# Linear attention and a routed expert layer on one core: a new explicit order for four engines and the transfers, and running counts in fewer, wider matmuls

## The chip, the cores and the metric

The kernel runs on one core of a Trainium2 chip. The core has a matrix engine (TensorE, PE in the profile), three further compute engines (VectorE or DVE, ScalarE or ACT, GpSimd or POOL) and SyncE (SP), which here only issues transfers. Each engine works through its own instructions in order; they wait for each other by semaphores. The metric is the device time of one execution in microseconds.

## The reference

Inputs are q, k, v, a_re, a_im of shape (4, 8, 768, 48), that is batch B, heads H, sequence S and head size D, and the weights of an expert layer with 8 experts, of which each token uses two.

```python
mag = np.sqrt(a_re * a_re + a_im * a_im)
scale = np.minimum(mag, 0.999) / (mag + 1e-06)
a_re_n, a_im_n = a_re * scale, a_im * scale
for t in range(S):                      # a complex decay of a state per head
    new_re = ar * S_re - ai * S_im
    new_im = ar * S_im + ai * S_re
    S_re, S_im = new_re + outer(k[t], v[t]), new_im
    y[t] = q[t] @ S_re
x = y as (B * S, H * D)                 # 3072 tokens of 384 numbers
noisy = x @ w_gate + log1p(exp(x @ w_noise)) * noise
top2, top2_w = the two largest of 8 and their softmax
for e in range(8):                      # w1[e]: 384 x 1024, w2[e]: 1024 x 384
    out[mask] += top2_w * (relu(x[mask] @ w1[e]) @ w2[e])
```

## The kernel before

The sequence is cut into chunks of 128 steps: 6 groups g of 4 tiles each (one tile per batch entry), so 24 tiles n = 0 to 23. The decay is split into a logarithm of its size and a phase. For each pair of tiles m the kernel loads a (S1, S2), takes logarithms and an arctangent (A1 to A5, D1 to D5), forms running sums by a triangular matmul (P1, P2), and sines and cosines (A7, A8). For each tile it scales q and k (D9 to D11), transposes them (P3, P4; copies A11, A12), forms scores (P5a, P5b; masked by D12a, D12b), the state update (P6, D13) and the output (P7a, P7b; copy A13), and transposes that back (P8, A14) into the rows `xr` of its group. Between groups the state is scaled by decay columns that make a round trip through DRAM (S5 out, S6 in as `ecol`; then D14, D15).

When a group's rows are there, the gates follow: logits (G0 to G3), noise and the two largest (G4 to G8), weights (G9, G12a to G12e), a running count of tokens per expert over the group's tiles (G10 on TensorE, G11a, G11b) and from it the slots `sl` (G12f, G12g). Then two indirect transfers per tile from GpSimd (L571 of the profile; L*bk.g* in the code: tile b, choice k, group g) scatter the rows of 1600 bytes to `xs` in DRAM, each expert's tokens side by side: eight scatters in groups 0 to 3. Groups 4 and 5 are cut in two parts, of three tiles and of one (4b, 5b). A copy of the group's rows also goes to `xd` (S13).

The expert part loads an expert's rows from `xs` (S14 for expert 0: the first 320 slots need groups 0 to 2 alone), transposes and splits them (P21, A23, D23), and runs two matrix products (P22 and P23) with weights loaded in pieces (S20, S22) and split into a rounded part and a rest on ScalarE and VectorE (A20, D20, A22, D22). Experts 1 to 7 follow at the end without an explicit order. Transfers that fill slots that may stay empty (S11, `xs<-none`, 300 KB each, eight) and clear the output (S12, `out_dram<-zero`, 384 KB each, twelve) can stand nearly anywhere ahead of their use.

Line 207 holds `ORDER`, a list of 1270 names in one line of time. A name is a step and its number: A is ScalarE, D VectorE, P TensorE, S a transfer on SP's queue; the G steps are on VectorE but for G0, G2, G10 (TensorE) and G1, G5, G7, G9 (ScalarE). Lines 960 to 964 take each engine's names in turn and make the first instruction of each follow the last of the one before. So the table sets the order inside an engine, not the times; and of a step with several instructions, such as the two S6 transfers, only the first has to stay behind the step before. The table ends with P23.02, expert 0's third output tile, and the few steps behind it.

`PACE` (line 526) names for most scatters one ScalarE step. The scatter waits until that step has run (line 948). The anchor is a lower bound: if the slots come later than the anchor, the scatter runs when the slots are there, in GpSimd's order.

```python
for d, n in behind:
    tc.add_manual_dep(d.ins, K[n][-1].ins.name, later, reason="pace")
```

Of the kernel before, what the change touches and what calls it, by code (L numbers as in the profile page):

```python
# [77 lines left out]
def kernel(  # L78
# [8 lines left out]
    nc = tc.nc  # L87
# [108 lines left out]
    def next_psc():  # L196
# [16 lines left out]
        D10.1 A11.0 S1.4 D11.1 P2.3 A2.2 P4.0 A1.3 D1.2 P6.0 A2.3 D2.2 S2.4 S7.1 A12.0 D1.3 S3.5 S6.1 A3.2
        P3.1 D13.0 A9.2 D3.2 P5a.0 A10.2 A9.3 D2.3 S5.2 P6.1 A4.2 S7.2 P5b.0 D9.2 S10.0 A3.3 A10.3 D3.3 A11.1
        D11.2 A4.3 S7.3 P4.1 S10.1 D13.1 S3.6 A0.3 D10.2 P6.2 S6.2 D12a.0 S2.5 A5.2 S4.3 P7a.0 A12.1 D5.2 A5.3
        D13.2 P1.4 S3.7 P1.5 D5.3 A6.4 S11.1 P3.2 A6.5 D7.4 D7.5 S7.4 P1.6 A11.2 D8.2 P1.7 D12b.0 A6.6 P4.2
        D9.3 A7.2 P7b.0 A6.7 D7.6 P5a.1 A8.2 S7.5 D7.7 S12.0 P5b.1 A13.0 D12a.1 S5.3 A12.2 S4.4 D8.3 P8.0 S3.8
        D12b.1 P7a.1 A7.3 S1.5 P5a.2 D4.2 A8.3 P7b.1 D10.3 P5b.2 A14.0 A0.4 D12a.2 P2.4 D12b.2 P3.3 A13.1
        D11.3 A9.4 P2.5 A11.3 S5.4 D4.3 P7a.2 S6.3 P7b.2 A10.4 A9.5 D9.4 S11.2 P8.1 A1.4 S4.5 P4.3 S7.6 A10.5
        D10.4 S12.1 A14.1 P2.6 A12.3 S5.5 D9.5 P2.7 S1.6 A13.2 D11.4 P3.4 A2.4 S6.4 D10.5 P5a.3 A11.4 S3.9  # L220
        D1.4 P5b.3 A9.6 A1.5 P4.4 D12a.3 S5.6 S4.6 A9.7 D12b.3 S2.6 P6.3 A2.5 D2.4 S1.7 P7a.3 A10.6 S7.7 D1.5
        A12.4 P7b.3 P8.2 S11.3 D9.6 A10.7 P3.5 S6.5 A14.2 A3.4 D11.5 S4.7 P5a.4 S3.10 A11.5 D2.5 P5b.4 S2.7
        A13.3 D3.4 P4.5 A3.5 S5.7 D12a.4 G0.0 A4.4 S11.4 D3.5 S12.2 A12.5 P7a.4 D12b.4 A4.5 D4.4 P5a.5 P5b.5
        A0.5 D10.6 P7b.4 D13.3 A5.4 D4.5 P8.3 P3.6 A13.4 D5.4 S8.5 G1.0 A14.3 S3.11 G2.0 A5.5 G3.0 P1.8 S8.4
        D12a.5 S6.6 P1.9 D5.5 A6.8 P6.4 A6.9 D7.8 A11.6 D7.9 P1.10 S4.8 D11.6 S12.3 A8.4 P1.11 S3.12 D13.4
        P4.6 A6.10 S11.5 D8.4 A6.11 D7.10 P6.5 A7.4 S6.7 D7.11 P7a.5 D12b.5 A12.6 D8.5 P7b.5 A8.5 D9.7 P5a.6
        A7.5 S4.9 D13.5 S12.4 D10.7 P8.4 A0.6 S3.13 P2.8 D11.7 P3.7 A14.4 G4.0 D12a.6 A9.8 P2.9 G5.0 A10.8
# [5 lines left out]
        S11.6 D13.7 P5a.8 A14.5 S7.10 A11.9 D11.9 S6.11 P6.8 G12d.0 A3.7 D10.10 P4.9 S7.11 A14.6 D12a.8 P8.7
        S3.15 A12.9 S12.6 D3.7 G0.1 S2.8 A15.2 A14.7 S4.11 D11.10 P5b.8 G1.1 S11.7 A4.7 G2.1 G12f.0 D12b.8
        P5a.9 A0.7 D14.1 P5b.9 G12e.0 S3.16 D15.4 G12g.0 P7a.8 G3.1 D4.6 A5.6 P7b.8 D12b.9 A5.7 D5.6 P3.10
        A13.8 D12a.9 P1.12 A11.10 D13.8 P1.13 D5.7 A6.12 P4.10 D15.5 A6.13 S3.17 D7.12 P7a.9 A12.10 S1.9 D15.6
        D7.13 P1.14 D9.11 A8.6 P7b.9 A6.14 D8.6 D10.11 P5a.10 A13.9 A7.6 D7.14 P1.15 D12a.10 P8.8 A6.15 D15.7
# [15 lines left out]
        A2.11 S5.18 D12a.15 S9.8 P3.16 A9.19 G8f.2 D12b.15 A10.19 S7.18 D13.14 P7a.15 A11.16 S5.19 G8g.2 D2.10
        S4.17 P7b.15 D9.19 P4.16 S6.18 A13.15 D10.17 A3.10 P8.13 S9.9 D1.11 G9.2 P6.15 A14.13 S13.1 A12.16
        G8h.2 G0.3 G12a.2 S7.19 D2.11 G10.2 D3.10 A3.11 P3.17 D11.17 A4.10 S6.19 P5a.16 G12b.2 A11.17 G11a.2
        D3.11 P5b.16 S4.18 S3.22 A15.4 D13.15 G1.3 P4.17 A4.11 G12c.2 G11b.2 D12a.16 G2.3 P8.14 A12.17 G3.3
        G12d.2 D10.18 P8.15 A0.11 S4.19 P5a.17 G12e.2 G12f.2 D14.3 P6.16 D15.12 A5.10 G12g.2 P7a.16 D12b.16
# [941 lines left out]
```

## Time and profile before

| | us |
|---|---|
| median of 3 runs | 689.98 |
| lowest and highest | 685.65 and 693.29 |
| the profiled execution | 692.53 |
| its span, first to last instruction | 690.7 |
| TensorE busy in the span | 641.5 |
| VectorE, ScalarE, GpSimd busy | 431.9, 327.3, 170.9 |

The profile is of one execution. Its views are the page (busy shares, the span in slices, the costliest groups), the busy time by stretch, the timeline of each engine, the list of waits, and the chain of work that ended last. A matmul's end is modelled, and matmuls overlap, so a TensorE that is shown as busy may still be slow. "Issue" as a releaser means that the engine waited for nothing that the profile shows. The span's first 295 us hold the attention, the gates and expert 0; the rest are the other experts.

### The profile page before, as it was taken

Reading aid. Unit: us, or ns where it says so; the run is one execution under the profiler, and the core shown is the slowest. Engines: PE = TensorE matmul, PEld = TensorE weight load, DVE = VectorE, ACT = ScalarE, POOL = GpSimd, SP = SyncE. Lnnn points to the kernel's source line nnn. Section 1 sums busy time; section 2 is a strip of 40 time slices with the busy share of each in tenths; the row PEclk is TensorE's granted clock in tenths of the full one; section 3 lists DMA queues with packets and bytes.
Section 4 is the critical chain, followed back from the end, with each engine's and each line's share of the span. In section 5 each row is a group of like instructions: output and inputs, shape, how many; then the busy total and the mean of one; then the engine's idle time right before and its main releaser. Section 6 shows DMA issues by size and latency. Waiting matters only on the chain.

```text
span 690.7 us, 13884 instructions
## 1 busy us (share of the span) xinstructions
PE 641.5 (93%) x5366; PEld 571.7 (83%) x5366; DVE 431.9 (63%) x946; ACT 327.3 (47%) x555; POOL 170.9 (25%) x185
## 2 busy tenths in 40 slices
PE   1789998898979998999999999999999999999995
PEld 0468786676858887879899899899899899899895
DVE  7899997787969756736454653734743744733311
ACT  7799986786865453234322521612521622512300
POOL 3000004131140623401422412412412512512311
PEclk9999999999999999999999999999999999999999
DMA  8468846583746656734645532833822742601201
GB/s 294 136 189 250 242 90 230 170 262 97 189 132 186 205 171 218 255 76 114 184 103 144 176 75 84 259 80 104 235 44 86 232 103 94 207 24 68 67 25 46
DMA packets 96680, 102.67 MB, mean 149 GB/s; under 512 B 60830, under 2 KB 77601, under 8 KB 96600
## 3 DMA queue, kind: packets, MB, share of 16 engines
q1 hardware_dynamic: 87240, 74.08, 39.0%
q0 software_dynamic: 9360, 27.54, 11.2%
q8 instruction: 48, 0.79, 0.5%
q14 instruction: 32, 0.26, 0.1%
HBM read 70.93 MB, written 31.70 MB: 149 GB/s over the span
## 4 chain that ended last, share of the span: by engine, by line
PE 81%; DVE 6%; issue 5%; DMA 3%; ACT 3%; POOL 1%; SPq 0%; POOLq 0%; DVEq 0%
PE po L810 28%; PE ph L760 28%; PE ptr L414 4%; PE psc L425 3%; PE cum L365 3%; PE pY L478 3%; PE pY L476 2%; PE cum L389 2%; PE pG L439 2%; PE po L816 2%; ACT t L296 2%; PE cum L491 1%; PE psc L760 1%; DVE qh L404 1%; DMA xgb<-xs 1%
## 5 line engine op out<-in xcount | busy, mean ns | idle before, releaser
L810 PE MATMUL po<-w2h,h 128*128 128x384 f32 x768 | 196.7, 334 | 0.0
L760 PE MATMUL ph<-x,w1h 128*128 128x512 f32 (+2 forms) x720 | 185.6, 346 | 0.8 <-ACT h L762 0.8
L760 PEld LDWEIGHTS ph<-x,w1h 128*128 128x128 f32 x720 | 126.2, 189 | 17.0 <-ACT h L762 1.0
L810 PEld LDWEIGHTS po<-w2h,h 128*128 128x128 f32 x768 | 138.9, 188 | 0.1
L810 PE MATMUL po<-w2l,h 128*128 128x384 f32 x384 | 128.3, 334 | 0.0
L760 PE MATMUL ph<-x,w1l 128*128 128x512 f32 (+2 forms) x360 | 124.6, 346 | 0.0
L822 POOL DMA_INDIRECT out_dram<-ao,ox x52 | 51.4, 988 | 251.7 <-DVE ao L821 225.5
L766 DVE SCALAR_TENSOR_TENSOR h<-ph,h 128x512 fp32r<-128x512 f32 (+2 forms) x144 | 69.9, 504 | 65.5 <-ACT h L762 60.7
L762 ACT ACTIVATE h<-ph 128x512 fp32r<-128x512 f32 (+2 forms) x120 | 60.5, 510 | 99.1 <-PE ph L760 96.3
L571 POOL DMA_INDIRECT xs<-xr,sl x48 | 56.8, 1182 | 171.4 <-ACT qT L415 105.5
L821 DVE SCALAR_TENSOR_TENSOR ao<-po,ex,ao 128x384 f32<-128x384 f32 (+1 forms) x42 | 25.8, 615 | 87.7 <-PE po L810 87.4
L686 ACT CAST w2h<-raw 128x768 fp32r<-128x768 f32 x32 | 26.5, 834 | 103.8 <-PE po L810 80.7
L760 PEld LDWEIGHTS ph<-x,w1l 128*128 128x128 f32 x360 | 67.9, 189 | 7.8
L810 PEld LDWEIGHTS po<-w2l,h 128*128 128x128 f32 x384 | 72.1, 188 | 0.1
L785 POOL DMA_INDIRECT ao<-out_dram,ox x49 | 55.7, 1136 | 42.8 <-issue 28.9
L478 PE MATMUL pY<-am,v 128*48 128x128 f32 x384 | 39.4, 284 | 5.4 <-DVE am L427 3.2
L425 PEld LDWEIGHTS psc<-qT,kT 112*64 112x64 f32 x768 | 37.2, 139 | 7.9 <-issue 6.5
L425 PE MATMUL psc<-qT,kT 112*64 112x128 f32 (+1 forms) x768 | 41.3, 253 | 1.6 <-issue 1.1
L741 ACT CAST x<-xt 128x512 fp32r<-128x512 f32 (+1 forms) x39 | 21.1, 545 | 41.5 <-DVE xt L740 37.8
L476 PE MATMUL pY<-qT,z 112*48 112x128 f32 x320 | 34.7, 288 | 5.3 <-DVE z L461 2.8
L687 DVE TENSOR_TENSOR w2l<-raw,w2h 128x768 fp32r<-128x768 f32 x32 | 30.3, 956 | 13.6 <-ACT w2h L686 10.9
L427 DVE TENSOR_TENSOR am<-psc,mask 128x512 f32<-128x512 f32 x48 | 32.6, 683 | 6.1 <-PE psc L425 4.7
(224 smaller groups left out, 934.1 us busy)
## 6 DMA issues: line engine op xcount, KB each, us to landing
raw<-in_moe_w_dram SPq DMA_DIRECT2D x24, 512.0 KB
raw<-in_moe_w_dram SPq DMA_DIRECT2D x32, 384.0 KB
qk<-in_qk_dram SPq DMA_DIRECT2D x24, 384.0 KB
v<-in_v_dram SPq DMA_DIRECT2D x24, 288.0 KB
xgb<-xs SPq DMA_DIRECT2D x28, 192.0 KB
out_dram<-zero SPq DMA_DIRECT2D x12, 384.0 KB
re<-in_a_dram SPq DMA_DIRECT2D x11, 384.0 KB
im<-in_a_dram SPq DMA_DIRECT2D x11, 384.0 KB
```

What stands on the lines that cost most here:

```text
L425: key(f"P5{'ab'[half]}.{n}", nc.tensor.matmul(p[o:o + 64, j, s:], KT[n][:, h, s:s + 64], QT[n][:, h, s:], start=True, stop=True, skip_grou ...
L427: LAST['am'] = nc.vector.tensor_mul(AM[n][:, 4 * half:4 * half + 4, :].rearrange("p (i r) t -> p i r t", r=2), p.rearrange("p (i r) t -> p ...
L476: x = nc.tensor.matmul(o, Z[b][:, h, :], QT[n][:, h, :], start=True, stop=False, skip_group_check=True)
L478: x = nc.tensor.matmul(o, V[n][:, H + i if r else h, :], AM[n][:, h, :], start=not g, stop=True, skip_group_check=True)
L571: d = key(f"L{b}{kk}.{part(g, lo)}", nc.gpsimd.indirect_dma_start(out=xs, out_offset=bass.IndirectOffsetOnAxis(ap=sl[:, kk, b:b + 1], axis=0),
L687: d = key(f"D{name}", nc.vector.tensor_tensor(lo, raw_t, hi.bitcast(F32), op=OP.subtract))
L760: LAST['m'] = key(f"P22.{e}{w}{f}", nc.tensor.matmul(p[:, :c], W1[e, kk][i][:, f * 128:(f + 1) * 128], XW[w, kk][:, j, 0:c], start=(m == 0 ...
L762: key(f"A24.{e}{w}{f}", nc.scalar.activation(h[:, 0:c], p[:, :c], AF.Relu))
L766: LAST['h'] = key(f"D25.{e}{w}{f}", nc.vector.scalar_tensor_tensor(h[:, dst:dst + b - a], p[:, a:b], 0.0, h[:, a:b].bitcast(F32), op0=OP.m ...
L785: nc.gpsimd.indirect_dma_start(out=ao[j][0:w, :], out_offset=None, in_=out, in_offset=bass.IndirectOffsetOnAxis(ap=OX[e][0:w, j:j + 1], ax ...
L810: LAST['po'] = key(f"P23.{e}{j}", nc.tensor.matmul(p[:, :DM], HT[w, f][i][:, o:o + 128], W2[f // 2][k2][:, f % 2, :], start=(m == 0), stop ...
L822: d = nc.gpsimd.indirect_dma_start(out=out, out_offset=bass.IndirectOffsetOnAxis(ap=OX[e][0:n, j:j + 1], axis=0), in_=a, in_offset=None, b ...
```

## The change

Three things change. `ORDER` has the same 1270 names in another order. `PACE` has other anchors, 35 instead of 34. And `gate_dispatch` forms the running counts by n + 1 matmuls instead of up to 14: the triangular one over all n tiles at once, then n of all ones, each over the tiles from 0 on and written j tiles further right, so that they add up in PSUM; the last block is the group's total.

```diff
@@ ORDER: a stretch around the slots of group 1, before and after
...
-        P2.14 S7.13 G8e.1 G8f.1 A14.10 D9.13 P3.12 A9.14 A10.14 G8g.1 P2.15 D10.13 A1.8 P5a.11 D9.14 G9.1 A2.8
-        S1.10 P5b.11 S4.13 G12a.1 A11.12 D12a.11 S6.12 P6.11 D1.8 A1.9 S7.14 P4.12 S3.19 D12b.11 A2.9 D2.8
...
-        S4.15 G0.2 A12.13 S3.20 D12b.12 P7a.12 G12d.1 A4.9 D10.14 P5a.13 D4.8 A0.9 P7b.12 G11a.1 D13.11 S12.9
-        G1.2 A5.8 G11b.1 P3.14 D12a.13 S6.14 G12f.1 A5.9 G12e.1 D5.8 G2.2 P6.12 A11.14 G12g.1 G3.2 P8.11
...
+        S1.10 D12a.11 P3.12 A14.9 G8h.1 G12c.1 D13.10 G10.1 P2.15 A11.12 S5.14 G11a.1 G12d.1 G11b.1 D16.1
+        S6.13 G12f.1 P8.10 G12e.1 G12g.1 D9.14 A1.9 P4.12 S13.1 S7.14 A2.9 D2.8 P5b.11 S4.14 A9.15 S3.18 D1.9
...
@@ PACE
-        "L01.0": "A14.4", "L10.0": "A4.7", "L11.0": "A12.9", "L20.0": "A6.13", "L21.0": "A6.14", "L30.0":
-        "A14.7", "L31.0": "A12.10", "L01.1": "A3.8", "L10.1": "A4.8", "L11.1": "A4.9", "L20.1": "A6.17",
-        "L21.1": "A13.12", "L30.1": "A6.19", "L31.1": "A6.19", "L01.2": "A12.16", "L10.2": "A4.10",
-        "L11.2": "A14.14", "L20.2": "A14.15", "L21.2": "A6.20", "L30.2": "A6.22", "L31.2": "A11.18",
...
+        "L01.0": "A4.6", "L10.0": "A12.9", "L11.0": "A14.7", "L20.0": "A6.13", "L21.0": "A13.9", "L30.0":
+        "A6.15", "L31.0": "A12.10", "L00.1": "A11.12", "L01.1": "A14.10", "L10.1": "A13.11", "L11.1":
+        "A11.13", "L20.1": "A14.11", "L21.1": "A4.9", "L30.1": "A6.17", "L31.1": "A6.18", "L01.2":
+        "A11.16", "L10.2": "A12.16", "L11.2": "A4.11", "L20.2": "A13.15", "L21.2": "A6.22", "L30.2":
+        "A6.23", "L31.2": "A6.20", "L01.3": "A23.001", "L10.3": "A23.002", "L11.3": "A11.20", "L20.3":
...
@@ def gate_dispatch(g, lo, hi, oh, ohs):
         p = psC.tile([128, 512], F32, name="cum")
-        for j in range(n + 1):
-            o = p[:, j * E:(j + 1) * E]
-            for i in range(min(j, n)):
-                key(f"G10.{part(g, lo)}", nc.tensor.matmul(o, ones_b, ohs[:, i, :], start=(i == 0), stop=(j == n and i == n - 1)))
-            if j < n:
-                key(f"G10.{part(g, lo)}", nc.tensor.matmul(o, tri_b, ohs[:, j, :], start=(j == 0), stop=True))
+        key(f"G10.{part(g, lo)}", nc.tensor.matmul(p[:, 0:n * E], tri_b, ohs.rearrange("p b e -> p (b e)"),
+                                                   start=True, stop=False, skip_group_check=True))
+        for j in range(1, n + 1):
+            key(f"G10.{part(g, lo)}", nc.tensor.matmul(p[:, j * E:(n + 1) * E], ones_b, ohs[:, 0:n + 1 - j, :].rearrange("p b e -> p (b e)"),
+                                                       start=False, stop=j == n, skip_group_check=True))
```

Of the transfers, the new table moves the fillers S11 and the clears S12 forward: up to the step P7b.0 of the old table stand S11.0 and S11.1; up to the same amount of TensorE work in the new one S11.0 to S11.4 and S12.0 to S12.4. The last filler, S11.7, moves from just ahead of G12g.0 to far ahead of it. The copies S13.0 to S13.2 come right behind their slots, S13.3 moves back behind most of group 4. S22.01 moves nearer to its cast A22.01, and S14.10, the load of the first rows of expert 1, moves back, nearer to its use.

## Rows read from the trace of the kernel before

**Rows 1.** The page, first block: busy time, share of the span and instructions of TensorE
```profile
PE 641.5 (93%) x5366; PEld 571.7 (83%) x5366; DVE 431.9 (63%) x946; ACT 327.3 (47%) x555; POOL 170.9 (25%) x185
```

**Rows 2.** Busy time by stretch: stretch, length, busy us (instructions) by engine, clock, DMA share, GB/s
```profile
0.00:46.00 46.00, 25.02 (x210) 15.63 (x212) 37.63 (x80) 36.45 (x62) 6.01 (x29) 0.96 0.67 207
46.00:93.00 47.00, 46.95 (x694) 38.80 (x694) 45.96 (x92) 45.72 (x76) 0.00 (x0) 1.00 0.78 222
93.00:107.00 14.00, 11.21 (x225) 10.07 (x225) 10.99 (x24) 11.58 (x19) 0.00 (x0) 1.00 0.51 116
107.00:130.00 23.00, 20.54 (x243) 15.38 (x240) 17.23 (x35) 13.74 (x23) 9.58 (x8) 0.93 0.47 174
...
148.00:166.00 18.00, 13.63 (x131) 9.85 (x130) 11.23 (x20) 10.30 (x18) 8.03 (x8) 0.91 0.42 124
...
187.00:210.00 23.00, 19.32 (x197) 13.95 (x194) 16.73 (x31) 15.40 (x27) 11.23 (x10) 0.93 0.42 135
...
227.00:253.00 26.00, 25.39 (x302) 23.78 (x301) 17.09 (x64) 13.05 (x25) 8.83 (x8) 1.00 0.64 204
253.00:268.00 15.00, 12.94 (x145) 10.56 (x142) 8.29 (x38) 5.70 (x16) 6.07 (x7) 0.89 0.47 153
...
295.00:690.00 395.00, 388.58 (x2170) 364.05 (x2169) 193.09 (x327) 120.30 (x203) 105.08 (x99) 1.00 0.41 114
```

**Rows 3.** Timeline of GpSimd: start, duration (us), line, operation, idle time before and releaser
```profile
112.31 1.17 POOL L571 DMA_INDIRECT xs<-xr,sl  x1 [105.50 <-ACT qT L415]
...
148.52 1.10 POOL L571 DMA_INDIRECT xs<-xr,sl  x1 [2.77 <-DVE lz L515]
...
157.71 0.98 POOL L571 DMA_INDIRECT xs<-xr,sl  x1 [0.30 <-issue]
...
187.06 3.79 POOL L571 DMA_INDIRECT xs<-xr,sl  x1 [3.63 <-DVE am L427]
...
199.05 0.98 POOL L571 DMA_INDIRECT xs<-xr,sl  x1 [0.30 <-issue]
...
223.78 4.53 POOL L571 DMA_INDIRECT xs<-xr,sl  x1 [21.51 <-DVE decm L452]
...
240.49 0.97 POOL L571 DMA_INDIRECT xs<-xr,sl  x1 [3.81 <-ACT kT L415]
```

**Rows 4.** Timeline of TensorE inside the second burst
```profile
157.10 0.27 PE L476 MATMUL pY<-qT,z 112*48 112x128 f32 x1 [1.09 <-issue]
...
158.53 0.31 PE L478 MATMUL pY<-am,v 128*48 128x128 f32 x1 [0.44 <-issue]
```

**Rows 5.** TensorE's waits from 223 to 243 us: total, times, longest
```profile
PE psc L760 <- issue: 0.4, 1, 0.4
```

**Rows 6.** The chain that ended last: start, duration (us), what
```profile
51.70 0.87 PE ptr L414 x8
...
101.34 4.06 DMA ecol<-es
```

**Rows 7.** Timeline of SP's transfer queue: issues
```profile
101.34 0.43 SPq L398 DMA_DIRECT2D ecol<-es  x1
...
103.88 1.09 SPq L899 DMA_DIRECT2D xs<-none  x1
...
201.79 0.50 SPq L617 DMA_DIRECT2D xga<-xs  x1
```

**Rows 8.** Timeline of VectorE around the first group's state update and slots
```profile
105.69 0.19 DVE L456 TENSOR_TENSOR fcol<-ecol,ecol 112x32 f32<-112x32 f32 x1 [2.68 <-DMA ecol<-es]
...
106.67 0.21 DVE L563 TENSOR_REDUCE sl<-ga4oh 128x8 uint32<-128x64 f32 x1
```

**Rows 9.** Timeline of TensorE: first and last of one group's running-count matmuls
```profile
219.96 0.18 PE L553 MATMUL cum<-ohs,tri_b 128*128 128x8 bf16 x1
...
220.22 0.24 PE L551 MATMUL cum<-ohs,ones_b 128*128 128x8 bf16 x4
```

**Rows 10.** Busy time by stretch, as in rows 2: the fullest 10 us of the queues
```profile
10.00:20.00 10.00, 5.81 (x8) 2.30 (x8) 7.31 (x16) 8.19 (x19) 0.00 (x0) 1.00 0.98 349
```

More of the change, by code (lines that the diff above doesn't have):

```diff
@@ L213 @@
[L213 to L227, printed above, removed]
@@ L233 @@
[L233 to L237, printed above, removed]
@@ L253 @@
[L253 to L257, printed above, removed]
@@ new lines @@
+        P2.23 G6a.3 D15.13 S14.00 A9.22 D9.21 P4.18 A10.22 S5.22 G6b.3 D13.16 P7a.17 G7.3 S12.10 A12.18 G6c.3
+        S4.18 D9.22 P7b.17 A9.23 G8a.3 D10.19 A10.23 P6.17 S5.23 A13.17 G8b.3 D9.23 S20.00 P3.19 G8c.3 D11.19
+        S12.11 P5a.18 A11.19 S6.20 G8d.3 P5b.18 D12a.18 S4.19 P4.19 G8f.3 D15.14 G9.3 G8e.3 G12a.3 P7a.18
+        G8g.3 A12.19 G12b.3 D15.15 G8h.3 D13.17 G10.3 P21.000 S20.01 G11a.3 G12c.3 D12b.18 P5a.19 A23.000
+        G12d.3 D23.000 P7b.18 G11b.3 S4.20 G12f.3 G12g.3 G12e.3 D10.20 P21.001 S6.21 A13.18 P6.18 A23.001
@@ new lines @@
+        D12a.19 A20.00 P5b.19 D23.001 D13.18 P21.002 D11.20 P6.19 A23.002 A20.01 S20.02 D23.002 P8.16 D10.21
+        P3.20 D11.21 P7a.19 A11.20 D20.01 G0.4 A14.16 P4.20 D12b.19 G1.4 D20.00 P7b.19 A12.20 D10.22 G2.4
+        A20.02 P3.21 D16.3 G3.4 D11.22 P8.17 A11.21 P8.18 G4.4 D20.02 A13.19 P4.21 G5.4 A14.17 D10.23 P22.000
+        D11.23 S22.00 P22.001 A24.000 G6a.4 D25.000 P22.002 A24.001 D25.001 G6b.4 P8.19 G7.4 A24.002 A14.18
+        P5a.20 D25.002 G6c.4 G0.4b G8a.4 P5b.20 D12a.20 G8b.4 P22.003 D12b.20 G8c.4 G8d.4 G8f.4 P22.004
@@ new lines @@
+        A24.003 A14.19 D25.003 G1.4b G9.4 G8e.4 A12.21 P22.005 S22.01 S6.22 A24.004 G2.4b A24.005 P7a.20 S4.21
+        G3.4b G8g.4 G4.4b G12a.4 G5.4b G6a.4b D25.004 P7b.20 D25.005 P5a.21 G6b.4b A13.20 G6c.4b G12b.4 P5b.21
+        G7.4b G8a.4b G8h.4 G8b.4b D12a.21 A22.01 S22.02 P3.22 S14.10 G10.4 P22.006 A11.22 G11a.4 G12c.4 S6.23
+        G12d.4 D12b.21 A22.00 S4.22 G8c.4b G12e.4 P4.22 D22.00 P7a.21 A12.22 G8d.4b G8e.4b G12f.4 G8g.4b
+        P7b.21 G8f.4b D13.19 A24.006 S22.03 G9.4b D22.01 S13.4 P3.23 A13.21 G12a.4b D25.006 P22.007 G12g.4
@@ new lines @@
+        S4.23 A11.23 P4.23 A24.007 D25.007 P5a.22 A12.23 S20.10 P5b.22 D12a.22 A22.03 P8.20 D12b.22 A22.02
+        P21.100 D22.03 P7a.22 A14.20 A23.100 D22.02 P7b.22 G12b.4b D23.100 P5a.23 A13.22 G11b.4 P5b.23 D12a.23
+        S20.11 G0.5 D14.5 G12c.4b D12b.23 P21.101 G1.5 P8.21 A23.101 G2.5 P7a.23 G3.5 G4.5 D23.101 G5.5 A14.21
+        G6a.5 P7b.23 G8h.4b G6b.5 G7.5 G6c.5 G12d.4b G8a.5 D16.4 G8b.5 G10.4b P21.102 G8c.5 G12e.4b A13.23
+        G11a.4b G8d.5 S13.4b P8.22 G11b.4b G8e.5 A23.102 S13.3 G12f.4b G0.5b G8g.5 A14.22 G12g.4b G8h.5
@@ L286 @@
+        D23.102 G1.5b G10.5 G8f.5 G2.5b D16.5 P23.00 G9.5 G12a.5 G3.5b G4.5b G5.5b G6a.5b G12b.5 G12c.5 G12d.5
+        G12e.5 S20.12 G11a.5 G12f.5 G6b.5b S13.5 G7.5b G6c.5b G12g.5 G8a.5b G8b.5b G8c.5b G8d.5b G8e.5b G8f.5b
+        G9.5b A20.10 G12a.5b G11b.5 D15.20 P8.23 A20.11 P23.01 D15.21 G12b.5b G8g.5b G8h.5b A14.23 D20.11
+        A20.12 G12c.5b D15.22 D20.10 G12d.5b G10.5b P23.02 G11a.5b G12e.5b G11b.5b G12f.5b S13.5b D15.23
+        G12g.5b D20.12 A28.02 D28.00 D28.01 D27.02 D28.02
     """.split()
```

100 lines of the change are left out of this document (51 added, 49 removed), and 5 rows, old and new, of the table PACE.

## The prediction

> **What bounds the kernel now.** I read the page's first block, then busy time by stretch, then the timelines of GpSimd and TensorE inside the stretches where busy time falls. TensorE is busy for 93% of the span [rows 1]. From 295 us on it waits for almost nothing (388.58 of 395 us) [rows 2], and the change touches nothing there: its table ends with the third output tile of expert 0. So only the first 295 us can move.
>
> In them, 46 to 93 is what the kernel looks like when the table fits: TensorE 46.95, VectorE 45.96 and ScalarE 45.72 of 47 us [rows 2]. No gain is left in such a stretch, because three engines are full at once. In 107 to 130, 148 to 166 and 187 to 210 all three fall together: VectorE is busy 17.23, 11.23 and 16.73 us of 23, 18 and 23 [rows 2]. GpSimd's timeline says what else runs there: the eight scatters of a token group, one behind the other, from 112.31 on, from 148.52 to 158.69 and from 187.06 to 200.03 [rows 3]. Inside such a burst TensorE issues single matmuls with 0.4 to 1.1 us between them and waits for nothing that the profile shows ("issue") [rows 4]. The granted clock of the same stretches is 0.93, 0.91 and 0.93 as a mean [rows 2]: after the halting matmuls a part of each runs at the lower level, 1.2 GHz, and 18 x 0.09 = 1.6 us of work is lost to it in the middle one.
>
> The control is group 3. Its eight scatters go from 223.78 to 241.46, 17.7 us instead of 10.2 [rows 3]; TensorE is busy 25.39 of 26 us in 227 to 253 at clock 1.00 [rows 2], and its only "issue" wait between 223 and 243 is 0.4 us [rows 5]. The same work, spread, costs nearly nothing. (TensorE issues fewer and longer matmuls there, which weakens the comparison.)
>
> **The change part by part. Scatters.** I walk along both tables and add up TensorE's turns at pitches of the trace: 0.87 us for eight transposes [rows 6], and likewise for the other kinds. This gives places in us of TensorE work, not times. From the entry that makes a group's slots (G12g) to the last anchor of its scatters (PACE), the old table has 7.2, 5.6 and 5.3 us for groups 0, 1, 2; the new one has 17.8 (65.1 to 82.9), 16.8 (93.5 to 110.3) and 14.7 (123.5 to 138.2). Group 3 has 15.6 before and 14.6 after. The slots come 8 to 13 us earlier than in the old table, so the anchors, and not the lateness of the slots, will set the spacing. Group 0 has one reason more: the last filler write of the slot table was issued at 103.88, the slots were ready at 106.88 and the first scatter ran only at 112.31 [rows 3, 7, 8], by when several anchors had passed. The new table puts that write 20.5 us of TensorE work before the slots, the old one 1.5.
>
> What it is worth: at VectorE's share of 46 to 93 (45.96/47 = 0.978) the 45.19 us of VectorE work in the three stretches need 46.2 us; they took 64. So 17.8 us are lost there, the clock's part included, and that is the upper bound; the lower is 0. I leave 1.6 us in each: the 0.6 us of TensorE idle time in group 3's stretch, and 1.0 because in every group two or three scatters still share nearly one anchor. Gain: **13.0 us**.
>
> **State columns.** At 105.69 VectorE had waited 2.68 us for a 1.5 KB transfer of decay columns, issued at 101.34 [rows 7, 8], and TensorE stood idle 2.79 us in 93 to 107 [rows 2]. From that transfer to its use the old table has 4.9 us of TensorE work, the new one 5.5, with the filler write gone from beside it. Bounds 0 and 2.8; the 0.6 us more and a freer queue give **1.0**.
>
> **Running counts.** In a group of four, 14 matmuls of 8 columns become 5 of 32 or fewer columns. The 14 start within 0.36 us, 26 ns each [rows 9]. Nine fewer in four groups and five fewer in the two groups of three are 46 x 26 ns = 1.2 us. If instead each wide one cost a 128-column transpose's 0.11 us (0.87/8, [rows 6]), 32 of them take 3.5 us where 78 took 2.0: 1.5 us lost. 32 columns of bf16 are nearer to the first row. Gain **0.8**.
>
> **Group 4, 253 to 268.** TensorE idles 2.06 us and loses 15 x 0.11 = 1.7 to the clock [rows 2]. Five of its six scatters keep nearly one anchor (188.9 to 193.2), as before. Gain 0 to 3.7; I take **0**.
>
> **Transfers at the start.** Up to the place that the kernel before reached at 46 us, the old table issues two filler writes (0.6 MB); the new one five, and five clears of the output (3.4 MB). The most that the queues moved is 349 GB/s [rows 10], so 2.8 MB are 8 us if nothing hides them. But the first 46 us averaged 207 GB/s [rows 2], which leaves room for (349 - 207) x 46 us = 6.5 MB. They stand ahead of loads on SP's one queue, so I charge **1.5** (bounds 0 and 8).
>
> **Loads nearer to their use.** One load of the second weight matrix (S22.01) is 3.3 us of work ahead of its cast, not 7.7, and group 3's 784 KB copy to DRAM moves behind most of group 4, where expert 0's last rows are awaited. The small transfer at 101.34 took 4.06 us to land [rows 6], so the first can be 0.8 us late on ScalarE with copies of later tiles queued behind it; the second is 784 KB / 349 GB/s = 2.2 us of queue time. Charge **1.0** (bounds 0 and 4).
>
> **Sum.** -13.0 - 1.0 - 0.8 + 0 + 1.5 + 1.0 = -12.3 us. The profiled execution took 692.53 us (span 690.7 and 1.8 around it): 680.2. The median of the runs, 689.98, is 2.55 lower: **678 us**.
>
> **Rivals.** *Everything smooth.* 46 to 93 shows what the table can reach; with the upper bounds, 17.8 + 2.8 + 1.2 + 3.7 = 25.5 us, the time is 664. Against it: the start and some clumps remain.
>
> *The spacing does not come about, or does not matter.* PACE gives only a lower bound to each scatter. If slots come 10 us late again, all anchors have passed and the burst returns; or each scatter costs TensorE its 0.55 us (4.4 idle us of 148 to 166 over eight) wherever it stands. Then of the 13 us about 2 remain: 689. For it: this happened to three groups before. Against: the slots' lead in the new table, and group 3.
>
> *Slow descriptors.* Single scatters took 3.79 and 4.53 us where most took 0.97 [rows 3], with VectorE busy all the time. The new table puts scatters into its fullest stretches. If all eight of group 2 took 3.79 + 0.3 us, they would end at 123.5 + 32.7 = 156.2 of work, and the load of expert 0's rows waits for them on SP (1.8 us after the last one, as at 201.79 [rows 3, 7]). With 4 us to land (the transfer of [rows 6]), the first transposes of the experts, placed at 152.6, would be 9.4 us late, and 1.6 to the clock: 690 - 12.3 + 11 = 689. Against it: in the dense stretch from 148.52 on the scatters took 0.97 to 1.10.
> The Trainium skill (SBUF — State Buffer, Who interferes with whom) states a rule for this: a transfer issued from GpSimd cannot get its descriptors written while VectorE holds the port pair that the two share in its two-port modes; its section on bandwidth pools gives about 3.1 us for one that takes 0.62 alone. By that figure the same sum ends at 150.7 and gives about 683. The trace agrees in two of the rows and not in the others.
>
> *Slower: each lone stall lowers the clock.* Today three groups of halts bring about one slow phase each, of 1.6 us. If spread scatters still halt TensorE 0.55 us each (13.2 in all against 10.5 of idle time now) and every second halt brings a slow phase, 12 x 1.6 = 19.2 replace 4.8: with the other terms (+0.7) 18 us more, 708. It becomes slower by 1% from six slow phases on. Against it: gaps of 0.4 us in group 3's stretch left the clock at 1.00.
>
> **How the numbers follow.** Forecast 0.56 (its own range 671 to 686, from the bounds of the start and of the scatters), smooth 0.14, no spacing 0.14, slow descriptors 0.06, clock 0.10. A measurement of this kernel can tell about 1% from no change, so faster means under 683: 0.49 of the forecast's 0.56 and 0.14, 0.63. Within 1%: the forecast's rest, 0.14 and 0.06, 0.27. Slower: 0.10. The range, 664 to 693, leaves out the clock case and the lower half of the smooth one.
>
> **What would show it.** Right: eight scatters of groups 0, 1 and 2 each over 14 us or more, no "issue" waits above 0.5 us on TensorE between 100 and 210, VectorE above 0.9 in every stretch from 107 to 210, and the output tiles of expert 0 some 12 us earlier. Wrong: scatters 1.28 us apart again; halts that remain though they are spread; the first 46 us longer by more than 2 us; SP waiting on the load of expert 0's rows; ScalarE waiting for weights.

## The result

The changed kernel took **671.54 us** as the median of four runs (668.92 to 672.65), the kernel before 690.07 beside it: a ratio of 0.973, 95% interval 0.967 to 0.979. Two more sets of runs, on two chips, gave 0.972 (0.963 to 0.981) and 0.971 (0.967 to 0.974). The prediction was 678 us with a range of 664 to 693. In place of the forecast gain of 12.3 us there came 18.5, or 19.8 between the spans of the two profiled executions (690.7 and 670.9).

The page of the changed kernel, its line of engines, as [rows 1]:

```profile
PE 633.5 (94%) x5320; PEld 566.6 (84%) x5320; DVE 430.5 (64%) x946; ACT 328.4 (49%) x555; POOL 175.1 (26%) x185
```

TensorE is busy 8 us less, in a span that is 20 us shorter. Its busy time by stretch, with the columns of [rows 2]:

```profile
46.00:93.00 47.00, 45.65 (x634) 36.51 (x635) 45.73 (x89) 45.82 (x77) 0.00 (x0) 1.00 0.78 221
93.00:107.00 14.00, 14.00 (x256) 12.69 (x256) 13.67 (x31) 11.92 (x19) 4.54 (x3) 1.00 0.92 294
107.00:130.00 23.00, 22.93 (x322) 18.69 (x319) 22.84 (x64) 21.22 (x37) 6.64 (x8) 1.00 0.49 148
...
148.00:166.00 18.00, 18.00 (x254) 14.62 (x249) 17.63 (x54) 17.48 (x33) 3.27 (x5) 1.00 0.58 139
...
187.00:210.00 23.00, 20.88 (x334) 18.16 (x331) 20.68 (x56) 12.30 (x20) 8.15 (x7) 1.00 0.87 255
...
227.00:253.00 26.00, 24.77 (x287) 21.81 (x286) 17.98 (x87) 13.27 (x28) 9.97 (x10) 1.00 0.68 233
253.00:268.00 15.00, 15.00 (x99) 14.84 (x98) 13.09 (x39) 4.55 (x10) 9.75 (x9) 1.00 0.78 265
268.00:276.00 8.00, 4.92 (x27) 4.60 (x26) 3.05 (x13) 2.27 (x5) 1.01 (x2) 0.79 0.59 168
```

In 107 to 130, 148 to 166 and 187 to 210 VectorE was busy 17.23, 11.23 and 16.73 us [rows 2]; now it is 22.84, 17.63 and 20.68, and the granted clock, 0.93, 0.91 and 0.93 before, is 1.00. The 2.8 us in which TensorE was idle in 93 to 107 are gone. Two rows are worse than what stood in their place: the first, where TensorE was busy 46.95 us before, and the last, the stop ahead of expert 0's last rows.

GpSimd's timeline, first and last scatter of groups 0 and 2 and the slowest one, as [rows 3]:

```profile
100.01 1.88 POOL L570 DMA_INDIRECT xs<-xr,sl  x1 [93.47 <-DMA im<-in_a_dram]
...
118.13 0.97 POOL L570 DMA_INDIRECT xs<-xr,sl  x1 [2.49 <-ACT ga4w L296]
...
159.97 0.99 POOL L570 DMA_INDIRECT xs<-xr,sl  x1 [10.21 <-DVE sl L562]
...
167.16 2.66 POOL L570 DMA_INDIRECT xs<-xr,sl  x1 [1.87 <-ACT t L296]
...
176.38 0.97 POOL L570 DMA_INDIRECT xs<-xr,sl  x1 [0.30 <-issue]
```

Group 0 takes 19.1 us, group 2 takes 17.4 (13.0 before), and both start earlier: 100 instead of 112, 160 instead of 187. TensorE's waits from 100 to 210 us, as [rows 5], hold no halting any more; the largest is a wait for VectorE's state update, and "issue" is down to one wait of 0.2 us:

```profile
PE pG L439 <- DVE z L446: 1.6, 2, 1.4
...
PE cum L365 <- issue: 0.2, 1, 0.2
```

What is left is in TensorE's timeline at the end of the table, the transposes of expert 0's last rows:

```profile
272.91 1.33 PE L734 MATMUL po<-ident,xgb 128*128 128x128 f32 x5 [3.08 <-DMA xgb<-xs]
```

### The profile page after: what moved, and what is told of

It is laid out like the page before. It is cut to its first block, busy times and chain, and to the rows that moved or that the text cites. A ratio compares the mean times of both kernels' runs of the same rounds, so it can differ in the third digit from the quotient of the medians.

```text
span 670.9 us, 13791 instructions
## 1 busy us (share of the span) xinstructions
PE 633.5 (94%) x5320; PEld 566.6 (84%) x5320; DVE 430.5 (64%) x946; ACT 328.4 (49%) x555; POOL 175.1 (26%) x185
## 4 chain that ended last, share of the span: by engine, by line
PE 58%; DMA 2%; POOL 0%; DVE 0%; issue 0%; POOLq 0%; SPq 0%
PE po L809 29%; PE ph L759 28%; PE po L815 1%; DMA xgb<-xs 1%; DMA out_dram<-ao,ox 1%; PE po L734 0%; POOL out_dram L821 0%; DVE ao L820 0%; POOLq L1145 0%; PE po L1001 0%; SPq L622 0%
## 5 line engine op out<-in xcount | busy, mean ns | idle before, releaser
L478 PE MATMUL pY<-am,v 128*48 128x128 f32 x384 | 36.5, 273 | 0.9 <-issue 0.4
L296 ACT ACTIVATE t<-t 128x768 f32<-128x768 f32 (+1 forms) x42 | 31.6, 763 | 1.8 <-DVE bad L339 1.7
```

The source lines that it names most:

```text
L296: phases[i].append(nc.scalar.activation(*args, **kw))
L478: x = nc.tensor.matmul(o, V[n][:, H + i if r else h, :], AM[n][:, h, :], start=not g, stop=True, skip_group_check=True)
```

## The experiments

The kernels ran in four sets; those of a set shared one chip and the runs of the kernel before. One thing must be known to read them: in the first set the kernel before took 674.88 us (19 runs), in the other three 690.59, 691.38 and 693.24, as in the prediction's profile. So each time is read against before of its own set. Theory 1, from the prediction: bursts of scatters halt TensorE (it stands between single matmuls, by "issue", again and again), and spacing them is what saves the time. Its rival: the new order of the engines saves it.

**e1_no_pace (first set): the changed kernel without anchors.**
```diff
     PACE = {
-        "L01.0": "A4.6", "L10.0": "A12.9", "L11.0": "A14.7", "L20.0": "A6.13", "L21.0": "A13.9", "L30.0":
...
     }
```


> The changed kernel with its table of anchors emptied: the order written for the four engines and the transfers stays the new one, the wider counts stay, but no scatter is tied to another instruction any more, so each group's eight scatters go as soon as their slots are written. Theory 1 (the spacing is what saves the time): the scatters of groups 0, 1 and 2 start 1.28 us apart again, TensorE halts again with gaps of 0.4 to 1.1 us that no semaphore explains, and the granted clock falls to half in windows between 100 and 210 us; of the 16.6 us gained between the first state product of tile 8 and expert 0's first product 8 to 15 us are lost, so about 680 to 687 us. Rival (the new order of the other engines saves the time, the spacing rides along): within 1% of the changed kernel, 667 to 677 us, with no new halts.


664.61 us, 0.988 of before (0.983 to 0.992). Both figures in us were worked out for a before of 690 us; against before's 674.88 a gain of 10.3 us is left without any anchor, as the rival has it.

**e2_spread_old (first set): the kernel before, new anchors for groups 0 to 2.**
```diff
-        "L01.0": "A14.4", "L10.0": "A4.7", "L11.0": "A12.9", "L20.0": "A6.13", "L21.0": "A6.14", "L30.0":
-        "A14.7", "L31.0": "A12.10", "L01.1": "A3.8", "L10.1": "A4.8", "L11.1": "A4.9", "L20.1": "A6.17",
...
+        "L01.0": "A12.10", "L10.0": "A13.9", "L11.0": "A6.15", "L20.0": "A7.7", "L21.0": "A10.12", "L30.0": "A11.11",
+        "L31.0": "A9.13", "L01.1": "A13.12", "L10.1": "A8.8", "L11.1": "A8.9", "L20.1": "A14.12", "L21.1": "A11.15",
...
```


> The kernel before with its own order and its own counts; only the anchors of the scatters of groups 0, 1 and 2 are drawn anew, each behind a ScalarE instruction that in the trace of before ended 1.8 to 3 us after the one of the scatter ahead, so that each group goes over 14 us or more. Groups 3 to 5 keep their old anchors. Theory 1 (the spacing saves the time): the halts of TensorE between 107 and 210 us and their clock windows go, 8 to 12 us faster than before, 678 to 682 us. Rival (the order saves the time): within 3 us of before, 687 to 693 us.


673.47 us, 0.9995 of before (0.997 to 1.002).

**e3_counts_only (first set): the kernel before with the new gate_dispatch.**
```diff
-        for j in range(n + 1):
-            o = p[:, j * E:(j + 1) * E]
...
+        key(f"G10.{part(g, lo)}", nc.tensor.matmul(p[:, 0:n * E], tri_b, ohs.rearrange("p b e -> p (b e)"),
+                                                   start=True, stop=False, skip_group_check=True))
...
```


> The kernel before with the new running counts alone: five wide products of a group accumulate in one bank in place of fourteen narrow ones. My price is 0.8 us less over six groups, 689 us, which can't be told from before by time; the trace should show the products of a full group at about half their time on TensorE and the columns of VectorE behind them unchanged. Rival (the accumulation over the same columns makes each product wait for the one ahead, or the group's slots come later): 0 to 1.5 us slower, with the slots of a group later behind its sums than before.


672.51 us, 0.997 of before (0.995 to 0.9998): 1.8 us less, the interval from 0.1 to 3.4. The five matmuls of group 3 in TensorE's timeline, which answer to [rows 9]:

```profile
206.26 0.19 PE L548 MATMUL cum<-ohs,tri_b 128*128 128x32 bf16 x1
206.30 0.24 PE L551 MATMUL cum<-ohs,ones_b 128*128 128x32 bf16 x4
```
From the first start to the last end they take 0.28 us; in [rows 9] the fourteen took 0.50. A 32-column one starts as soon after the one ahead as an 8-column one did. The term's price of 26 ns holds, and the slower bound falls.

The first two spoke for the rival: here the order, with the new counts and without any anchors, was worth 10 us and the spacing nothing. But the trace of e3_counts_only, whose scatters stand in the old bursts, has no halts at all. GpSimd's timeline, the first and the last scatter of its group 1:

```profile
141.54 1.10 POOL L570 DMA_INDIRECT xs<-xr,sl  x1 [1.70 <-DVE lz L515]
...
151.09 1.41 POOL L570 DMA_INDIRECT xs<-xr,sl  x1 [0.31 <-issue]
```
The busy time of the stretch around them:

```profile
141.00:153.00 12.00, 12.00 (x150) 8.72 (x149) 11.84 (x22) 11.47 (x21) 8.83 (x8) 1.00 0.66 193
```
Eight scatters in 11 us, and TensorE is busy 12.00 of 12 us. In this set there was nothing for the spacing to save. (Before itself has no profile here; its 674.88 us leaves no room for halts either.) So the next set put the kernel before, the changed one and the one without anchors side by side.

**r1_before and r2_after (second set): both kernels, unchanged; e1b_no_pace: the kernel of e1_no_pace again.**


> The kernel before, unchanged, with a profile of its own beside the others of this call. The kernels made from it by a change of anchors or of counts ran in 673 us on their chip and showed scatters 1.28 us apart with no halts, where the profile that the prediction read has halts in three bursts and 690 us. Theory 2 (the halts are not made by the burst but come and go with the chip): where before takes about 675 us here, its profile shows the bursts of groups 0, 1 and 2 at 1.28 us with fewer than three gaps of TensorE over 0.4 us inside them, and its longest gap between 150 and 215 us is one of 3 to 5 us at the first load of expert 0's rows. Theory 1 (bursts make halts): halts of 0.4 to 1.1 us in all three bursts, whatever the time.

> The changed kernel, unchanged. If the halts come with the chip (theory 2), the gain here is that of e1_no_pace against before, 7 to 14 us less than before, since neither has halts to lose. Theory 1: 15 to 22 us less than before, as on the chip of the first profiles.

> The changed kernel with its table of anchors emptied, again, now beside the changed kernel itself. Theory 1 (the spacing saves the time): 8 us or more slower than the changed kernel. Theory 2 (the order saves it and the anchors are at best neutral): equal within 3 us, or up to 4 us faster, because no scatter waits for an anchor and the loads of expert 0's rows come earlier by the time that groups 2 and 5 save.


r1_before 691.21 us, r2_after 672.20 (0.972), e1b_no_pace 686.90 (0.996, 0.991 to 1.0005). Here the halts are there, in the same burst of the same code. The stretch of r1_before's second burst:

```profile
149.00:161.00 12.00, 8.47 (x81) 5.18 (x80) 6.85 (x11) 8.69 (x13) 8.11 (x8) 0.86 0.55 173
```
And the timeline of TensorE's weight loads in it:

```profile
156.71 0.12 PEld L478 LDWEIGHTS pY<-am,v 128*48 128x48 f32 x1 [0.62 <-issue]
157.40 0.12 PEld L478 LDWEIGHTS pY<-am,v 128*48 128x48 f32 x1 [0.57 <-issue]
158.13 0.15 PEld L478 LDWEIGHTS pY<-am,v 128*48 128x48 f32 x1 [0.61 <-issue]
158.84 0.15 PEld L476 LDWEIGHTS pY<-qT,z 112*48 112x48 f32 x1 [0.55 <-issue]
```
TensorE issues one weight load every 0.69 to 0.73 us, though each takes 0.12 to 0.15. And without its anchors the changed kernel halts too, in the stretches of its groups 1, 2 and 4:

```profile
130.00:148.00 18.00, 15.22 (x233) 11.63 (x229) 12.52 (x18) 11.89 (x17) 8.51 (x9) 1.00 0.67 222
...
166.00:187.00 21.00, 18.46 (x273) 13.87 (x271) 18.93 (x39) 18.40 (x28) 10.78 (x10) 1.00 0.60 194
...
227.00:253.00 26.00, 22.70 (x264) 20.10 (x264) 12.93 (x53) 13.47 (x25) 5.84 (x6) 0.90 0.37 127
```
So theory 1 holds where before takes 690 us, theory 2 where it takes 675: the same burst halts TensorE in some sets and not in another. With halts the anchors are worth 686.9 - 672.2 = 14.7 us.

**e5_pin_xga (second set): the kernel before with one line.**
```diff
+            tc.add_manual_dep(ds[1].ins, ds[0].ins.name, mybir.DependencyInfo(mybir.DependencyClass.NoSync, mybir.DependencyReason.DATA), reason="second piece")
             first.extend(ds)
```


> The kernel before with one line: the second piece of the load of expert 0's first rows (64 rows) is tied behind the first piece on SP. In before it is bound by nothing and lands ahead of three small transfers and one load of q and k on SP's queue, where it waits for group 2's last scatter (185.08 to 201.79 us in the first profile) with all of these behind it. Theory 3 (this wait stops the stages ahead of expert 0, and the new order removes it by bringing group 2 forward): TensorE's gap of 3 to 5 us there falls below 1 us and its clock does not fall, 3 to 6 us faster than before. Rival (the wait only moves to the first piece): within 2 us of before.


689.68 us, 1.0005 of before (0.996 to 1.005): the rival's time, though not by its reason. SP's queue shows why, here in e5_pin_xga:

```profile
185.32 0.40 SPq L568 DMA_DIRECT2D xd<-xr  x1
202.11 0.25 SPq L396 DMA_DIRECT2D es<-ee  x1
```
The load is no longer in front, and SP waits as long, for a small transfer whose source ScalarE forms only after the halts. Whether the line helps where there are no halts wasn't tried.

**e2b_spread_old (third set): the kernel of e2_spread_old, where there are halts; r3_after: the changed kernel beside it.**


> The kernel of e2_spread_old again: the kernel before with only the anchors of groups 0, 1 and 2 drawn anew, for a chip on which before shows halts. Where before takes about 690 us, theory 1 (spacing removes the halts): 8 to 12 us less than before, no gaps of TensorE over 0.5 us inside the three groups. Rival (the old order halts anyway, whatever the spacing): within 3 us of before. Where before takes about 675 us both expect no difference, as e2_spread_old showed.

> The changed kernel, unchanged, as the measure for e8_both. On a chip where before takes about 690 us: 671 to 673. On one where before takes about 675 us, so without halts: theory 2 says 663 to 668, since the order alone gave e1_no_pace 10 us there and the anchors then have nothing to save; if the change were all spacing, 673 to 676.


e2b_spread_old 678.30 us, 0.981 of before (0.975 to 0.986): 13.1 us less, from anchors alone. r3_after 670.10, 0.971 (0.967 to 0.974). By stretch, e2b_spread_old:

```profile
107.00:130.00 23.00, 21.39 (x246) 15.24 (x244) 19.34 (x48) 17.04 (x30) 10.03 (x8) 1.00 0.54 186
148.00:166.00 18.00, 18.00 (x270) 14.84 (x269) 17.84 (x47) 16.92 (x31) 9.22 (x7) 1.00 0.66 165
166.00:187.00 21.00, 19.32 (x309) 15.80 (x308) 18.97 (x46) 19.11 (x28) 8.03 (x7) 0.98 0.62 192
```
Group 1, in 148 to 166, is smooth. In groups 0 and 2 five scatters still stood in a row, since the first one came late and took long (2.97 and 3.79 us), so that the anchors of the next had passed; there some halts remain.

**e7_far_burst (third set): is it GpSimd's work or the bytes?** The changed kernel with this behind group 0's scatters, where `far` holds a number beyond the table, so that these eight write nothing:
```diff
+        for b in range(8 if g == 0 else 0):
+            d = nc.gpsimd.indirect_dma_start(
+                out=xs, out_offset=bass.IndirectOffsetOnAxis(ap=far, axis=0),
+                in_=XR[g][:, b % 4, :], in_offset=None, bounds_check=E * N - 1, oob_is_err=False)
...
+            behind.append((d, PACE["L31.0"]))
```


> The changed kernel with eight more scatters of group 0's rows behind group 0, all with slot numbers beyond the table, so that they write nothing; they are tied to the anchor of group 0's last scatter and follow it at once. GpSimd does the work of a burst, the queues move none of its bytes. On a chip with halts: if GpSimd's own work makes TensorE halt, gaps of 0.3 us or more come in 120 to 131 us, from about the sixth scatter on; if the 1.6 MB that eight scatters move do it, that stretch keeps TensorE's 23 of 23 us. On a chip without halts nothing is told.


683.10 us in one run, 13.0 more than r3_after. The transfer queue that GpSimd fills, in the burst of r1_before (148 to 161 us): packets, MB, share of the queues' time.

```profile
q0 software_dynamic: 512, 1.64, 32.6%
```
The same in the burst of e7_far_burst (119 to 130):

```profile
q0 software_dynamic: 512, 0.21, 7.0%
```
As many packets, an eighth of the bytes; those are the one real scatter among the nine, at 125.08 us. The halts begin before it, at 122. Busy time by stretch of e7_far_burst:

```profile
107.00:130.00 23.00, 19.08 (x243) 14.18 (x238) 15.49 (x30) 16.17 (x27) 15.19 (x13) 0.93 0.34 106
130.00:148.00 18.00, 17.48 (x238) 14.79 (x238) 14.96 (x45) 12.51 (x20) 4.30 (x6) 0.80 0.60 174
```
One of its halts, in TensorE's timeline:

```profile
126.80 0.37 PE L478 MATMUL pY<-am,v 128*48 128x128 f32 x1 [0.95 <-issue]
```
The changed kernel beside it (r3_after) had 23.00 of 23 us at clock 1.00 there. A burst that moves hardly any bytes halts TensorE as well, so the traffic isn't the cause. Whether GpSimd's work or the handling of its packets is, this run doesn't separate. Behind it the clock spent a while at 1.2 GHz (0.93 and 0.80 as means of the two stretches).

**e8_both (third set): two transfers moved, for a better kernel.** In the changed kernel group 3's copy S13.3 goes from behind S13.4b to behind S14.10, with the line of e5_pin_xga.
```diff
@@ ORDER, the names of SP alone
-S22.02 S14.10 S6.23 S4.22 S22.03 S13.4 S4.23 S20.10 S20.11 S13.4b S13.3 S20.12
+S22.02 S14.10 S13.3 S6.23 S4.22 S22.03 S13.4 S4.23 S20.10 S20.11 S13.4b S20.12
```


> The changed kernel with two of its transfers moved: group 3's 784 KB copy to DRAM goes ahead of most of group 4, right behind the load of expert 1's first rows (about 209 us instead of 245 us, the queues moved 3 GB/s or less from 215 to 225 us), and the second piece of the load of expert 0's first rows is tied behind its first. Theory (the last scatters land behind this copy, and expert 0's last rows are late by it): the gap before the transposes of these rows falls from 2 to 3 us to under 1 us, its slow clock phase goes, and the gap of 1.3 us near 199 us falls too: 2 to 4 us less than the changed kernel. Rival (the rows are late because of the scatters' own time): within 1 us of it.


672.96 us beside the changed kernel's 670.10, ratios to before 0.972 (0.968 to 0.976) and 0.971: 2.9 us more, with ranges that overlap, so no gain. Its SP queue:

```profile
209.33 0.58 SPq L560 DMA_DIRECT2D xd<-xr  x1
...
265.52 0.33 SPq L616 DMA_DIRECT2D xgb<-xs  x1
```
And TensorE's timeline where the rows are used:

```profile
272.61 1.76 PE L728 MATMUL po<-ident,xgb 128*128 128x128 f32 x7 [3.35 <-DMA xgb<-xs]
```
The copy left 36 us earlier and the rows came no sooner. They wait for the last scatter itself, which ended on GpSimd at 261.6: 4 us until the load can be issued, 7 more until its rows are used. The gap near 199 stayed too (1.41 us); in the changed kernel it is a wait for VectorE's state update (1.4 us), not for a transfer.

**e9_spread_more (fourth set): how far do anchors alone go?** The anchors of groups 0, 2 and 4 drawn again from e2b_spread_old's trace.
```diff
@@ PACE, against e2b_spread_old
...
-    "L30.1": "A10.17", "L31.1": "A10.18", "L01.2": "A14.15", "L10.2": "A6.21", "L11.2": "A8.10", "L20.2": "A8.11",
+    "L30.1": "A10.17", "L31.1": "A10.18", "L01.2": "A6.21", "L10.2": "A6.23", "L11.2": "A7.11", "L20.2": "A9.20",
...
```


> The kernel of e2b_spread_old with the anchors drawn once more from its own trace: there group 0 still began with five scatters in a row, group 2 with five (TensorE halting four times by 0.4 us at 183.5 to 186, then a slow clock phase of 3.4 us) and group 4 with five (1.9 us of gaps from 242.8 on). Now the scatters of groups 0, 2 and 4 stand 1.3 to 3 us apart at least; order and counts stay those of before. On a chip where before takes about 690 us: theory 1 (spacing is nearly all of the change) says 4 to 7 us less than e2b_spread_old, so 0.972 to 0.976 of before, as good as the changed kernel's 0.971. Rival (the rest of the gain comes from the new order of the other engines): 0.979 to 0.983, as e2b_spread_old.


678.87 us, 0.981 of before (0.977 to 0.985): the rival's number. Of its reason, the new order, one point can be read in the trace: when the slots come. The halts of group 2 are gone. In their place there is a new wait. GpSimd's timeline, the last scatter of group 2:

```profile
192.23 2.73 POOL L570 DMA_INDIRECT xs<-xr,sl  x1 [0.30 <-issue]
```
SP's queue, the load of expert 0's rows behind it:

```profile
196.73 0.34 SPq L615 DMA_DIRECT2D xga<-xs  x1
```
TensorE's timeline, its next matmul:

```profile
200.14 0.88 PE L734 MATMUL ptr<-ident,xga 128*128 128x128 f32 x3 [6.20 <-DMA xga<-xs]
```
Up to there this kernel is level with the changed one: both begin the output of tile 18 at 189.5 us (r3_after). Then TensorE stands 6.2 us, because a group that goes out from 174.18 on and is spread ends too late, at 194.96, for the load of expert 0's rows; expert 0 begins 9 us behind the changed kernel (200.1 and 190.7). The changed kernel sends group 2 from 159.97 on (its rows above), and issues the load at 179.3.

The ratios to the kernel before of the same set:

| | old order | new order |
|---|---|---|
| halts in before: scatters in bursts | 1.001 (r1_before) | 0.996 (e1b_no_pace) |
| halts in before: scatters spaced | 0.981 (e2b, e9) | 0.971 (r3_after) |
| no halts: scatters in bursts | 1 | 0.988 (e1_no_pace) |
| no halts: scatters spaced | 1.000 (e2_spread_old) | not run |

The new order's column holds the new counts and the moved transfers as well, and its bursts are those of a kernel without any anchors. The counts alone gave 0.997 (e3_counts_only), and the interval of 0.996 reaches 1.0005, so the new order in bursts, where there are halts, is not clear of no gain.

## Why the prediction was right, and where it was off

The working's steps against the two profiles (before and after), split where the same output tiles begin; together the parts make the 19.8 us between the spans.

| Part | Forecast gain | Measured |
|---|---|---|
| start, up to tile 7's output | -1.5 | -1.8 (93.3 to 95.1 us) |
| state columns, tile 7 to tile 8 | 1.0 | 3.1 (13.5 to 10.4) |
| scatters and counts, tile 8 to expert 0's first product | 13.0 + 0.8 | 16.6 (120.4 to 103.8) |
| group 4, to the end of the table | 0 | 4.0 (54.0 to 50.0) |
| loads, behind the table | -1.0 | -2.1 |

**The mechanism of the main term was right.** It said that the burst halts TensorE, that the halts drag VectorE and the clock down, and that spacing gives it back. e2b_spread_old changes the anchors alone and gains 13.1 us, e1b_no_pace loses 14.7 when they go, and e7_far_burst makes the same halts by a burst put into a smooth stretch. The signs that were named came: groups spread over 17 us and more, no "issue" wait above 0.5 us, VectorE at 0.99, 0.98 and 0.90 of the three stretches (the last, 20.68 of 23, just under the mark), expert 0's output tiles earlier (by 21 us, not 12).

**Its control was misread.** The prediction calls group 3's scatters spread, from the first and the last of them. The rows between show a row of seven from 223.78 on, six of them close together, and one scatter behind. GpSimd's timeline, and the busy time of that stretch:

```profile
228.62 0.98 POOL L571 DMA_INDIRECT xs<-xr,sl  x1 [0.30 <-issue]
...
235.70 0.98 POOL L571 DMA_INDIRECT xs<-xr,sl  x1 [0.31 <-issue]
```
```profile
228.00:237.00 9.00, 8.65 (x98) 7.89 (x96) 6.03 (x25) 2.83 (x9) 6.85 (x7) 1.00 0.87 287
```
So group 3 doesn't show that spread scatters cost nothing. It shows a burst that does not halt TensorE, beside expert 0's products. That spacing helps in groups 0 to 2 rests on e1b_no_pace and e2b_spread_old, not on this control.

**The main term was sized too low, by 2.8 us at most.** Its part was forecast at 13.8 us, counts included, and measured 16.6. The step that was off is "I leave 1.6 us in each": between 100 and 210 us the only "issue" wait left is one of 0.2 us. But not all of the 16.6 us need be spacing. In the first of the three stretches of the kernel before, the clock was down at its lower level early:

```profile
108.00:112.00 4.00, 4.00 (x26) 3.21 (x22) 3.73 (x6) 1.46 (x2) 0.00 (x0) 0.57 0.99 391
```
That is ahead of the first scatter, at 112.31, and behind the 2.8 us in which TensorE stood idle for the state columns [rows 2]; the prediction laid it to "the halting matmuls". So up to 1.7 us (4 x 0.43) of the 16.6 can come from the end of that wait, and e3's 1.8 us (0.1 to 3.4) from the counts. The 13 to 15 us that are left agree with the 13.1 of e2b_spread_old and the 14.7 of e1b_no_pace. (In r1_before the slow phase of this stretch does follow the halts.)

**Start.** That -1.8 came for -1.5 is partly luck. In the first 46 us TensorE now waits 1.2 us for loads of v, which it did not before; two waits of 0.6 us for VectorE, at 73 and 76 us, are new too and have nothing to do with transfers.

**State columns.** "0.6 us more and a freer queue give 1.0" was too careful; the wait went altogether, and the measured 3.1 us are a little above the 2.8 of idle time that was the bound.

**Group 4 at 0 was wrong.** The step was "five of its six scatters keep nearly one anchor, as before". In places of work they do. In time four came in a row from 231.49 to 236.44, then two from 238.49 on, where before five stood in a row from 253.05 with 2 us of gaps and a slow clock phase behind them [rows 2]. In the traces with halts the repeated gaps begin when two to five scatters of a row have been started, so one fewer can matter but need not; why this group went better was not tested.

**Loads: the size was near, the cause was not.** The charge was laid on S13.3 being late. e8_both moves it away and the stop stays. Group 5's scatters and the way of the last one to DRAM set that time; TensorE reaches this point sooner after the end of that scatter (7.7 us, 9.0 before) and so waits longer (3.08 us here, 1.97 and 2.39 in the two repeats, 1.49 before), with a slow phase behind it (clock 0.79 in 268 to 276).

**What the prediction did not see.** First, that the two halves of the change need each other. It used the slots' lead to argue that the anchors would set the spacing, and gave the load's wait for group 2's last scatter to a rival with slow descriptors alone. e9_spread_more shows the other use of the lead: spacing makes a group's last scatter later, and the load of expert 0's rows waits for that one. Without the earlier slots the gain stops at 13 to 14 us; without the spacing the gain of order and counts is 3.7 us where there are halts, not clear of none. Second, that the halts are not in every set: with none of them, order and counts without anchors gave 10.3 us.

**The rivals.** "The spacing doesn't matter" is what the first set shows, on a chip without halts; in the three others it falls. "Each lone stall lowers the clock" falls: outside the first 46 us the changed kernel has one slow phase ahead of the last experts, behind its longest stop, where before had four. "Slow descriptors": in groups 0 to 2 of the changed kernel, with VectorE busy nearly always, the scatters took 0.97 to 1.88 us but for one of 2.66, and the load of expert 0's rows was there in time. Long scatters go with what VectorE does beside them: over eight of the traces (both kernels, their three repeats, e1b, e3 and e9), of 87 scatters longer than 1.3 us 82 overlapped by more than 0.6 us with TENSOR_TENSOR or SCALAR_TENSOR_TENSOR instructions that read two tiles of SBUF; of 240 shorter than 1.0 us it was 45. The longest, 4.53 us from 223.78 in the kernel before, had such instructions beside it nearly all the time, as this one in VectorE's timeline:

```profile
225.09 2.36 DVE L687 TENSOR_TENSOR w1l<-raw,w1h 128x1024 fp32r<-128x1024 f32 x2
```
The rule that the prediction takes from the Trainium skill (SBUF — State Buffer, Who interferes with whom) is for VectorE's two-port modes. The same section of the Trainium skill says that `tensor_tensor` has none, but that with both inputs in SBUF it contends with what GpSimd reads; the long scatters fit this, and not the rule that was cited for them. That VectorE makes them long was not tested.

**What stays open.** Why a row of scatters keeps TensorE from issuing, and why it didn't in the first set, can't be told from these runs. That the first set differs by its chip is likely but not shown, since its chip was seen in that set alone; the chip of the third and fourth sets showed halts in both. The changed kernel itself was not run where there are no halts; e1_no_pace gives 0.988 for its order and counts there.

## What to carry to other kernels

Look in GpSimd's timeline for several indirect transfers in a row, and see whether TensorE's issue gets slow beside them; if so, tie each to a step of another engine, about 2 us apart. But first make their indices early: the last one ends later when they are spread, and whatever loads the result waits for it. Profile the kernel before on more than one chip before a stall is called a property of the code.

## What the runs showed of the hardware

A row of indirect transfers from GpSimd, started about 1.28 us apart, slowed the issuing of TensorE's instructions to about one weight load per 0.70 us (r1_before, 156.71 to 158.84). The repeated gaps began when two to five of a row had been started, mostly three to five, and ended within some 2 us of the start of its last. The profile shows no semaphore behind them, and hardly any bytes had to move (0.21 MB against 1.64).

A row is not enough for it. Every row that halted TensorE again and again stood beside the attention's short matmuls. Rows beside expert 0's products did not: seven from 223.78 in the kernel before (TensorE busy 8.65 of 9 us in 228 to 237), and eight from 250.62 to 262.1 us of the changed kernel (15.00 of 15 us in 253 to 268). That the length of the matmuls decides is not shown. And it is not always there: in one set of runs bursts of eight at 1.28 to 1.7 us left TensorE busy 12.00 of 12 us, and the kernel before took 675 us instead of 690.
